# Attention and a gated feed-forward layer on one core: a third accumulator bank, scores in the accumulator ring, and new planned times

## The chip, the cores and the metric

The kernel runs on one core of a Trainium2 chip. The metric is device time in microseconds (us), from the start to the end of one execution. The kernel before takes 516.85 us, the median of three runs (515.93, 516.85 and 517.66).

## The reference

The reference takes q, k and v of shape 8 x 8 x 576 x 64 (batch, heads, positions, head width) and computes attention in a window: position i sees the positions i-63 to i. The heads are then laid side by side (512 wide) and go through a layer with two matrix products, a convolution of three taps along the positions, and a gate:

```
scores = q k^T / 8, masked to 0 <= i - j < 64;  attn = softmax(scores) v
x = attn, heads side by side             # 8 x 576 x 512
h = relu(x w_in)                         # 512 -> 1024
c = conv_w[0] h[i-1] + conv_w[1] h[i] + conv_w[2] h[i+1]
out = (h * sigmoid(c)) w_out             # 1024 -> 512
```

q and k are scaled by about 6.2, so the scores are not small. w_in, conv_w and w_out come as 64-bit floats, and the kernel converts them to 32 bits on the chip.

## The kernel before, in words

**Units and slots.** The 4608 positions are cut into 12 units of 384. A unit's inner width of 1024 is cut into 8 blocks f of 128. Planned times are in slots: one slot is one f, and unit u begins at slot 8u.

**Work of a unit.** Scores and softmax of a unit come in three groups b of four blocks (`softmax`, L477; the first two units are handled by `scores` and `weigh`, L449 and L460, in six pairs). TensorE computes scores (`qk`, L362, matmuls at L372), VectorE adds the mask and takes the row maximum (L379), ScalarE takes exponentials (L389), then they are normalised (L400), transposed by VectorE (L426), and put in place by DMAs (L438) or, for the first two units, transposed by TensorE (L405). `values` (L519, matmuls at L523) multiplies by v for one c of four; ScalarE and VectorE take the result out of PSUM as a high part xh (L527) and a low part xl (L530).

The first product, `mm1` (L540, matmuls at L543), adds up 12 matmuls of 384 columns for each f (high and low parts of x and w_in) in one bank. `relu` on ScalarE (L569 or L572) empties the bank into hbuf. For pairs i of two f the convolution runs on ScalarE (L578) and VectorE (L585), then sigmoid (L592), gate (L597), and the split into high and low parts gh (ScalarE, L609) and gl (VectorE, L612). The second product, `mm2` (L615, matmuls at L620), adds up over all f into three banks po0 to po2, nine matmuls of 512 columns for each f. The result is copied out (L660, L662) and stored (L666).

**Front.** Before this is in steady state the weights must be there: `weights` (L265) loads a chunk of 512 KB (L271), and ScalarE, VectorE and GpSimd convert it (L257 to L263) and split it into a high and a low part (L278 to L281). w_in comes in five steps, w_out in four of two f each. `keep_busy` (L215) puts matmuls that compute nothing (L220) where the planner expects TensorE to be idle in the first 110 us.

**PSUM.** There are eight banks: sc0 and sc1 for scores, acc0 and acc1 as a ring for `values` and `mm1`, and po0 to po3. `bank` (L513) gives the ring's banks in turn, in order of planned time. po3 is used for the first two units alone: transposes and score pairs (`PE_AT`, `QK_AT`, `bank_of` at L355).

**Order.** Each piece of work is put in a list with a planned time, an engine, a cost, and what it reads and writes (`at`, L226). The list is sorted by planned time, which sets the dependencies. Then `queued` (L65) goes through it once, when the kernel is built: it keeps a clock for each engine and, when an engine is free, takes of the pieces that its costs say are ready the one with the earliest planned time (0.5 slot earlier for one of the same kind as the last). The outcome is a fixed order of instructions on each engine. On the chip every engine works through its list in that order, and an instruction that waits holds all that stand behind it. Landing of a DMA is reckoned at L129 and L130. The planned times are in `START` (L145): `lag` is how many slots mm2 comes behind mm1, `qk` the three score groups, `pv` the four values groups, `in` and `out` the conversions of weights.

Of the kernel before, what the change touches and what calls it, by code (L numbers as in the profile page):

```python
# [8 lines left out]
F32 = mybir.dt.float32  # L9
# [6 lines left out]
P = 128  # L16
# [8 lines left out]
NU = B * S // NX  # L25
NG = NX + 2
TT = NX // P
NC = DM // P
NF = DFF // P
BY_PE = 2  # L30
NB = 4
# [3 lines left out]
GROUPS = ((0, 1), (2,), (3,), (4, 5))  # L35
QK_AT = (((-1,), (0,), (2,), (-1,), (0,), (2,)), ((-1,), (2,), (-1,), (2,), (-1,), (2,)))
PE_AT = ((0, 1, 2, 3, 0, 1), (0, 1, 0, 1, 0, 1))
MASKED = -8.0e9


# [24 lines left out]
def queued(works, fill=None):  # L65

    import heapq
    writer, readers = {}, {}  # L70
    for x in works:
        deps = set()
        for k in x.r:
            if k in writer:
                deps.add(writer[k])
        for k in x.w:
            deps.update(readers.get(k, ()))
            if k in writer:
                deps.add(writer[k])
        deps.discard(x)  # L80
        for d in deps:
            d.after.append(x)
        x.needs = len(deps)
        for k in x.w:
            writer[k], readers[k] = x, []
        for k in x.r:
            readers.setdefault(k, []).append(x)
    free = {"PE": 0.0, "DVE": 0.0, "ACT": 2.0, "POOL": 0.7, "SP": 0.75}
    state = dict.fromkeys(free)
    state["ACT"] = "exp"  # L90
    waiting = {e: [] for e in free}
    touched = {k: ("", 0.0) for k in [("sc", 0)] + [("acc", i) for i in range(2)] + [("po", i) for i in range(NC)]}
    for x in works:
        if x.needs == 0:
            waiting[x.eng].append(x)
    dma, port, order, left = 0.0, {"DVE": 0.0, "POOL": 0.0}, [], len(works)
    while left:
        best = None
        for e, ws in waiting.items():
            if not ws:  # L100
                continue
            start = max(free[e], min(x.ready for x in ws))
            if best is None or start < best[0]:
                best = (start, e)
        start, e = best
        x = min((x for x in waiting[e] if x.ready <= start),
                key=lambda x: x.t - (0.5 if x.kind and x.kind == state[e] else 0.0))
        if x.port:
            if e == "POOL" and start < port["DVE"]:
                free[e] = port["DVE"]  # L110
                continue
            start = max(start, port["POOL"])
            port[e] = start + x.port
        waiting[e].remove(x)
        if fill and e == "PE" and start < FILL_TO:
            t = max(free[e], FILL_FROM)
            n = int((start - t) * (FILL if start > COLD else 2.2))

            clean = [(end, k) for k, (by, end) in touched.items() if by != "PE" and end < t]
            if n > 0 and clean:  # L120
                order.append(Work(x.t, e, 0.0, fill(n, min(clean)[1]), [], [], None, 0, 0.0))
        turn = SWITCH[e] if e in SWITCH and (x.kind != state[e] if e == "PE" else x.kind and x.kind != state[e]) else 0.0
        if turn and e == "PE" and not x.kind:
            turn = LEAVE
        if e == "PE" or x.kind:
            state[e] = x.kind
        end = free[e] = start + turn + x.cost * (1.75 if e == "PE" and start < WARM else 1.0)
        if x.mb:
            dma = max(dma, start) + x.mb * 2.45  # L129
            end = dma + 2.1  # L130
        for k in x.r + x.w:
            if k[:2] in touched:
                touched[k[:2]] = e, end
        order.append(x)
        left -= 1
        for y in x.after:
            y.needs -= 1
            y.ready = max(y.ready, end + (0.0 if e == "PE" else 0.06) if y.eng == e else end + 0.2)
            if y.needs == 0:
                waiting[y.eng].append(y)  # L140
    return order
# [1 line left out]


START = {  # L145
    "v0": -75.194,
    "pv0": -28.294,
    "conv": -20.578,
    "bits": ((-108.97, -51.701), (-77.864, -72.033)),
    "qk1": -71.549,  # L150
    "lag": (17.427, 16.64, 17.098, 17.112, 17.608, 17.66),
    "mid": (4.229, 1.343, 1.083, 1.035),
    "v1": -24.291,
    "qk2": -12.096,
    "qk0": (-94.127, -93.129, -92.414, -87.931, -71.603, -79.477),
    "ex0": (-20.247, -71.357, -69.778, -64.052, -53.337, -51.735),
    "sc1": (-51.518, -55.088, -50.832, -25.283, -23.913, -20.247),
    "ex1": (-104.146, -25.732, -3.586, -17.027, -68.77, -2.709),
    "mask": -25.382,
    "sig": ((11.515, 14.523, 14.512, 21.442), (14.628, 17.367, 17.217, 19.829), (12.924, 15.579, 19.8, 20.604), (13.999, 15.174, 19.801, 20.222)),  # L160
    "in": (-24.969, -18.475, -6.673, -3.797, 1.924),
    "out": (7.771, 12.189, 12.98, 14.058),
# [3 lines left out]
}  # L166
SWITCH = {"PE": 0.14, "ACT": 1.28}
LEAVE = 0.24
# [7 lines left out]
def attention_moe(ctx: ExitStack, tc: tile.TileContext, q, k, v, w_in, conv_w, w_out, out):  # L176
# [30 lines left out]
    w24 = [flat[:, 8 * NT * 32:8 * NT * 32 + 2 * DM], flat[:, 16 * NT * 32:16 * NT * 32 + 2 * DM]]  # L207
    cbits = pool.tile([P, 3 * NF, 2], U32, name="cbits")
    sc = many(2, [P, 512], F32, "sc", psum)
    acc = many(2, [P, 512], F32, "acc", psum)  # L210
    po = many(NC, [P, 512], F32, "po", psum)

    spare = pool.tile([P, P], F32, name="spare")

# [140 lines left out]
    def bank_of(u, b, i, h):  # L355

        if not wide(u):
            return sc[h][:, i * P:(i + 1) * P]
        j = pair(u, NB * b + i)
        return (sc[h] if j < 0 else po[j + h])[:, i % 2 * P:(i % 2 + 1) * P]  # L360

# [115 lines left out]
    def softmax(u, b, t, ex_at):  # L477
        for i in range(NB):
            if block(u, b, i)[1]:
                at(t - 0.1, "POOL", 0.2, lambda b=b, i=i: nc.gpsimd.memset(ss[b][:, i, :, :W], 0.0), w=[("s", b, i)])  # L480
        at(t, "PE", 0.82, lambda b=b: qk(u, b), r=needed(b), w=[("sc", 0)], kind="eight")
        at(t + 0.002, "DVE", 1.45, lambda b=b: row_max(u, b),
           r=[("sc", 0), "mask1", "mask2"], w=[("s", b, i) for i in range(NB)] + [("nm", b, i) for i in range(NB)])
        t = ex_at
        for i in range(NB):
            at(t, "ACT", 0.74, lambda b=b, i=i: exps(u, b, i), r=[("nm", b, i)],
               w=[("s", b, i), ("sm", b, i)], kind="exp")
        t += 0.45
        e = slice(0, 2 * NB)
        sw, sr = [("sm", b, i) for i in range(NB)], [("s", b, i) for i in range(NB)]  # L490
        if u < 3:
            at(t, "POOL", 0.6, lambda: guard(b, e, nc.gpsimd), w=sw)
        else:
            at(t, "DVE", 0.15, lambda: guard(b, e, nc.vector), w=sw)
        at(t, "DVE", 0.15, lambda: reciprocal(b, e), r=sw, w=[("r", b, i) for i in range(NB)])
        if u < 3:
            two(t, "DVE", 0.88, lambda: normalise(u, b, e, nc.vector), r=[("r", b, i) for i in range(NB)], w=sr)
        else:
            two(t, "POOL", 1.5, lambda: normalise(u, b, e, nc.gpsimd), r=[("r", b, i) for i in range(NB)], w=sr)
        t += 0.4  # L500
        t = max(t, when[-1][2] + 0.1)
        for g, t0, rows in parts(b):
            at(t, "DVE", 0.12 * 2 * len(rows), lambda b=b, g=g, t0=t0, rows=rows: transpose(b, g, t0, rows), r=sr,
               w=[("T", g)] + ([("w24", 0, 0), ("w24", 0, 1)] if g else []))
            if t0 + len(rows) == NT:
                if u == BY_PE:
                    at(t + 0.01, "POOL", 1.0, lambda g=g: zero_blocks(g), w=[("u", g, i) for i in range(4)])
                for i in range(4):
                    at(t + 0.05, "SP", 2.1, lambda g=g, i=i: place(g, i), r=[("T", g)], w=[("u", g, i)], mb=0.15)
# [2 lines left out]

    def bank(key):  # L513
        if key not in banks:
            banks[key] = turn[0] % 2
            turn[0] += 1
        return banks[key]

# [191 lines left out]
            load_v(n0 + NF - 0.3, u + 2)  # L710
    load_qk(START["qk2"], 2)
    plan.sort(key=lambda x: x.t)
    for x in plan:
        x.r = [("acc", bank(a[1])) if type(a) is tuple and a[0] == "acc" else a for a in x.r]
        x.w = [("acc", bank(a[1])) if type(a) is tuple and a[0] == "acc" else a for a in x.w]

    kind = None
    for x in plan:
# [65 lines left out]
```

## Time and profile before

| what | value |
|---|---|
| median of 3 runs | 516.85 us |
| profiled execution | 521.77 us, span 520.0 us |
| TensorE busy | 503.5 us (97%) |
| VectorE, ScalarE, GpSimd busy | 370.4, 382.9, 88.9 us |
| mean granted TensorE clock | 0.993 |
| DMA | 69.89 MB, 134 GB/s in the mean |

TensorE's busy time includes the matmuls that compute nothing (16.6 us by their records). Matmuls overlap in the records: a record's length is longer than the distance between the starts of two matmuls, and the distance is what one costs. PEclk is the share of the full TensorE clock that was granted.

### The profile page before, as it was taken

The page shows a single profiled execution, that of the slowest core. Times are in us where ns is not written, and L with a number is a line of the kernel's source. Part 1 is how long each engine was busy: PE and PEld are TensorE (multiplying, and loading weights), DVE is VectorE, ACT ScalarE, POOL GpSimd, SP SyncE. Part 2 cuts the span into 40 slices and gives each one's busy share as a digit, 9 for nine tenths or more (in the row PEclk, how much of TensorE's full clock was granted, in tenths as well). Part 3 has the DMA queues.
Part 4 walks back from the last instruction along what each step waited for, and adds up shares of the span by engine and source line. Part 5 has one row for each costly group of instructions (what it writes and reads, how often), then busy time and mean ns, then how long its engine had stood idle before and what let it go on. Part 6 is the DMA issues. An engine that isn't in the chain of part 4 may idle for free.

```text
span 520.0 us, 14061 instructions
## 1 busy us (share of the span) xinstructions
PE 503.5 (97%) x5434; PEld 448.4 (86%) x5434; DVE 370.4 (71%) x1079; ACT 382.9 (74%) x1010; POOL 88.9 (17%) x196
## 2 busy tenths in 40 slices
PE   8898979999999999999999999999999999999996
PEld 7777979799988989989988988989889889898885
DVE  5889968898866667757766775775865865554970
ACT  6988958979877877777868868859769757644750
POOL 7213301221111112111103104203102201000000
PEclk9999979999999999999999999999999999999999
DMA  8983853436422542542551461452352231200111
GB/s 300 351 315 121 311 188 109 143 116 219 161 78 63 199 146 70 190 150 51 198 161 46 147 216 47 142 190 77 136 179 84 77 104 27 81 0 1 61 62 61
DMA packets 28163, 69.89 MB, mean 134 GB/s; under 512 B 5696, under 2 KB 15680, under 8 KB 28096
## 3 DMA queue, kind: packets, MB, share of 16 engines
q1 hardware_dynamic: 28096, 68.99, 39.7%
q8 instruction: 43, 0.70, 0.5%
q14 instruction: 24, 0.20, 0.1%
HBM read 47.73 MB, written 9.44 MB: 110 GB/s over the span
## 4 chain that ended last, share of the span: by engine, by line
PE 84%; DMA 9%; SPq 2%; DVE 2%; ACT 1%; issue 1%; ACTq 0%
PE po L620 38%; PE acc L543 34%; PE acc L523 6%; PE sc L372 5%; DMA q<-in_q_dram 4%; DMA bits<-in_w_out_dram 2%; SPq L438 1%; DMA bits<-in_w_in_dram 1%; DMA v<-in_v_dram 1%; SPq L243 1%; PE po L220 1%; DVE T L263 0%; ACT s L389 0%; DMA ub<-T 0%; DVE s L400 0%
## 5 line engine op out<-in xcount | busy, mean ns | idle before, releaser
L543 PE MATMUL acc<-xh,wih 128*128 128x384 f32 x384 | 131.7, 343 | 3.2 <-ACT hbuf L569 3.2
L543 PE MATMUL acc<-xl,wih 128*128 128x384 f32 x384 | 130.4, 339 | 0.0
L543 PE MATMUL acc<-xh,wil 128*128 128x384 f32 x384 | 130.0, 339 | 0.0
L585 DVE SCALAR_TENSOR_TENSOR c<-hbuf,cw,c 128x384 f32<-128x384 f32 (+1 forms) x192 | 117.5, 663 | 14.0 <-ACT c L578 13.4
L620 PE MATMUL po<-woh,gh 128*128 128x512 f32 x288 | 115.6, 401 | 0.0
L620 PE MATMUL po<-wol,gh 128*128 128x512 f32 x288 | 113.3, 394 | 0.0
L620 PE MATMUL po<-woh,gl 128*128 128x512 f32 x288 | 112.2, 389 | 0.0
L389 ACT ACTIVATE s<-s,nm 128x96 f32<-128x96 f32 (+2 forms) x288 | 105.0, 369 | 2.3 <-DVE nm L379 2.0
L543 PEld LDWEIGHTS acc<-xh,wih 128*128 128x128 f32 x384 | 73.1, 190 | 7.4 <-ACT hbuf L569 3.5
L612 DVE TENSOR_TENSOR gl<-c,gh 128x768 fp32r<-128x768 f32 x48 | 46.8, 976 | 44.1 <-ACT gh L609 44.0
L543 PEld LDWEIGHTS acc<-xh,wil 128*128 128x128 f32 x384 | 73.1, 190 | 2.6
L400 POOL TENSOR_TENSOR s<-s,r 128x768 f32<-128x768 f32 x27 | 41.8, 1546 | 195.1 <-DVE r L395 127.1
L543 PEld LDWEIGHTS acc<-xl,wih 128*128 128x128 f32 x384 | 72.9, 190 | 0.0
L620 PEld LDWEIGHTS po<-woh,gl 128*128 128x128 f32 x288 | 54.1, 188 | 12.2
L620 PEld LDWEIGHTS po<-woh,gh 128*128 128x128 f32 x288 | 54.0, 187 | 10.8
L578 ACT ACTIVATE c<-hbuf,cw 128x384 f32<-128x384 f32 (+1 forms) x96 | 53.6, 610 | 10.4 <-DVE gl L612 10.3
L620 PEld LDWEIGHTS po<-wol,gh 128*128 128x128 f32 x288 | 54.2, 188 | 7.7
L609 ACT CAST gh<-c 128x768 fp32r<-128x768 f32 x48 | 39.9, 831 | 25.7 <-PE po L620 21.4
L597 DVE TENSOR_TENSOR c<-c,hbuf 128x768 f32<-128x768 f32 (+1 forms) x48 | 45.1, 951 | 17.4 <-ACT c L592 17.1
L379 DVE CUSTOM_DVE_ANT_0 s<-sc,mask 128x96 f32<-128x96 f32 (+2 forms) x260 | 49.1, 253 | 8.2 <-PE sc L372 6.8
L389 ACT ACTIVATION_READ_ACCUMULATOR s<-s,nm 128x1 f32 x288 | 54.9, 191 | 0.0
L572 ACT ACTIVATE hbuf<-acc 128x384 f32<-128x384 f32 x64 | 31.1, 486 | 29.3 <-PE acc L543 28.9
(64 smaller groups left out, 557.9 us busy)
## 6 DMA issues: line engine op xcount, KB each, us to landing
v<-in_v_dram SPq DMA_DIRECT2D x24, 768.0 KB, 5.7
ub<-T SPq DMA_DIRECT2D x240, 48.0 KB, 1.9
k<-in_k_dram SPq DMA_DIRECT2D x22, 448.0 KB, 3.7
q<-in_q_dram SPq DMA_DIRECT2D x22, 384.0 KB, 5.1
out_dram<-T SPq DMA_DIRECT2D x11, 768.0 KB, 3.6
bits<-in_w_in_dram SPq DMA_DIRECT2D x8, 512.0 KB, 6.9
bits<-in_w_out_dram SPq DMA_DIRECT2D x8, 512.0 KB, 6.8
k<-in_k_dram SPq DMA_DIRECT2D x2, 256.0 KB, 5.3
```

The source lines that it names most:

```text
L379: nc.vector.tensor_tensor_reduce(out=ss[b][:, i, h, o:n], in0=bank_of(u, b, i, h)[:, o:n], in1=mask[m][:, o:n], scale=-0.125, scalar=3.0e3 ...
L389: nc.scalar.activation(x, x, AF.Exp, bias=nms[b][:, e], scale=-1.0, accum_out=sms[b][:, e])
L400: on.tensor_tensor(sv, sv, rs[b][:, e].unsqueeze(2).broadcast_to([P, e.stop - e.start, n]), ALU.mult)
L523: nc.tensor.matmul(acc[bank(("v", u, c))][h * D:(h + 1) * D, t * W:(t + 1) * W], vs[:, c, t, h], ub[g][:, 2 * p:2 * p + 2, 2 * t + h], sta ...
L543: nc.tensor.matmul(acc[bank(("m", u, f))][:, :NX], w[:, f, c], x[u % 2][:, c], start=(c == 0 and j == 0), stop=(c == NC - 1 and j == 2))
L572: nc.scalar.activation(hbuf[:, f, 1:1 + NX], ps[:, :NX], AF.Relu)
L578: nc.scalar.activation(cs[i % 2][:, a, :n], hbufs[u % 2][:, f, 1:1 + n], AF.Copy, scale=cw[:, 1, f:f + 1])
L585: nc.vector.scalar_tensor_tensor(c, hbufs[u % 2][:, f, e:e + n], cw[:, e, f:f + 1], c, op0=ALU.mult, op1=ALU.add)
L597: nc.vector.tensor_tensor(c, c, hbufs[u % 2][:, 2 * i:2 * i + 2, 1:1 + n], ALU.mult)
L609: nc.scalar.copy(halves(u, ghs[ring(u, i)]), kept(u, cs[i % 2]))
L612: nc.vector.tensor_tensor(halves(u, gls[ring(u, i)]), kept(u, cs[i % 2]), halves(u, ghs[ring(u, i)]).bitcast(F32), ALU.subtract)
L620: nc.tensor.matmul(po[t], x, w[:, f], start=(f == 0 and j == 0), stop=(f == NF - 1 and j == 2))
```

## The change

The ring gets a third bank, acc2, and po loses its fourth. Where po3 was used, in the first two units, the same place is now acc2, and the planner knows it as such. The second group of scores (b = 1) of each unit from the third on is written into two banks of the ring, taken in turn like the others; the first and third groups stay in sc0 and sc1. The planner reckons a DMA's landing later. All planned times in `START` are new (cut to those that the text speaks of). No instruction of the computation is added or taken out; `keep_busy` matmuls are placed anew by the planner.

```
+NA = 3
+IN_ACC = (1,)
 in queued():
-    touched = {... for k in [("sc", 0)] + [("acc", i) for i in range(2)] + [("po", i) for i in range(NC)]}
+    touched = {... for k in [("sc", 0)] + [("acc", i) for i in range(NA)] + [("po", i) for i in range(TT)]}
...
         if x.mb:
-            dma = max(dma, start) + x.mb * 2.45
-            end = dma + 2.1
+            dma = max(dma, start) + x.mb * 2.6 + (0.15 if x.mb > 0.2 else 0.0)
+            end = dma + 2.4
...
 START:
-    "bits": ((-108.97, -51.701), (-77.864, -72.033)),
-    "lag": (17.427, 16.64, 17.098, 17.112, 17.608, 17.66),
-    "in": (-24.969, -18.475, -6.673, -3.797, 1.924),
-    "out": (7.771, 12.189, 12.98, 14.058),
-    "pv": (..., (3.533, 3.36, 7.02, 7.429)),
-    "qk": ((-7.026, 4.948, -1.256), (6.222, 6.805, 7.164), (4.422, 4.464, 6.363), (3.571, 7.538, 11.237)),
+    "bits": ((-258.913, -43.524), (-27.85, -45.73)),
+    "lag": (14.24, 14.398, 15.694, 15.676, 15.748, 15.604),
+    "in": (-109.707, -10.794, -9.091, -3.35, 0.324),
+    "out": (1.022, 7.827, 9.957, 12.645),
+    "pv": (..., (5.736, 6.769, 6.475, 6.894)),
+    "qk": ((4.51, 3.967, 5.895), (7.399, 7.175, 7.913), (5.253, 4.827, 5.309), (5.703, 5.416, 6.817)),
...
-    acc = many(2, [P, 512], F32, "acc", psum)
-    po = many(NC, [P, 512], F32, "po", psum)
+    acc = many(NA, [P, 512], F32, "acc", psum)
+    po = many(TT, [P, 512], F32, "po", psum) + acc[2:]
 in bank_of():
-            return sc[h][:, i * P:(i + 1) * P]
+            tile = acc[bank(("s", u, b, h))] if b in IN_ACC else sc[h]
+            return tile[:, i * P:(i + 1) * P]
 in softmax():
-        at(t, "PE", 0.82, lambda b=b: qk(u, b), r=needed(b), w=[("sc", 0)], kind="eight")
+        where = [("acc", ("s", u, b, h)) for h in range(2)] if b in IN_ACC else [("sc", 0)]
+        at(t, "PE", 0.82, lambda b=b: qk(u, b), r=needed(b), w=where, kind="eight")
         (row_max reads `where` as well)
 in bank():
-            banks[key] = turn[0] % 2
+            banks[key] = turn[0] % NA
 before the planner runs:
+    def place_in(k):
+        if type(k) is not tuple:
+            return k
+        return ("acc", bank(k[1])) if k[0] == "acc" else ("acc", 2) if k == ("po", 3) else k
```

## Rows read from the trace of the kernel before

**Rows 1.** The page's first part: busy time, share of the span, instructions.
```profile
PE 503.5 (97%) x5434; PEld 448.4 (86%) x5434; DVE 370.4 (71%) x1079; ACT 382.9 (74%) x1010; POOL 88.9 (17%) x196
```

**Rows 2.** Windows: length, then busy time by engine, PEclk, DMA share, GB/s.
```profile
30.00:40.00 10.00, 7.86 (x121) 7.07 (x120) 9.06 (x44) 8.61 (x37) 2.71 (x4) 1.00 0.76 278
40.00:50.00 10.00, 8.91 (x192) 8.26 (x192) 8.86 (x27) 8.34 (x24) 2.78 (x4) 1.00 0.31 108
...
60.00:70.00 10.00, 7.81 (x143) 7.03 (x141) 6.64 (x24) 4.36 (x10) 2.64 (x6) 1.00 0.83 278
70.00:80.00 10.00, 9.01 (x35) 9.01 (x36) 9.16 (x11) 8.46 (x12) 1.76 (x4) 0.66 0.58 196
...
250.00:290.00 40.00, 40.00 (x460) 35.68 (x459) 26.86 (x86) 29.78 (x78) 5.97 (x9) 1.00 0.41 132
```

**Rows 3.** Timeline of TensorE, first wait: start, length, what [idle before, releaser].
```profile
37.26 0.60 PE L405 MATMUL po<-ident,s 128*128 128x128 f32 x4
41.09 0.99 PE L372 MATMUL sc<-k,q 64*32 64x96 f32 x64 [3.23 <-DMA q<-in_q_dram]
```

**Rows 4.** Timeline of TensorE, second wait and the matmuls behind it.
```profile
67.47 0.34 PE L543 MATMUL acc<-xl,wih 128*128 128x384 f32 x1
70.99 0.69 PE L543 MATMUL acc<-xh,wih 128*128 128x384 f32 x1 [3.18 <-ACT hbuf L569]
...
76.91 0.48 PE L543 MATMUL acc<-xh,wih 128*128 128x384 f32 x1
```

**Rows 5.** Chain of waits, merged: start, length, what; two units, 40 us apart.
```profile
272.61 2.11 PE acc L543 x12
274.71 2.06 PE po L620 x9
...
312.55 2.11 PE acc L543 x12
```

**Rows 6.** Timeline of ScalarE: a relu of unit 0, and the queue around 69.43.
```profile
39.18 0.47 ACT L572 ACTIVATE hbuf<-acc 128x384 f32<-128x384 f32 x1
...
69.43 1.12 ACT L257 ACTIVATE T<-bits 128x1024 f32<-128x1024 f32 x1 [5.53 <-DMA bits<-in_w_out_dram]
70.45 0.49 ACT L569 ACTIVATE hbuf<-acc 128x384 f32<-128x384 f32 x1
```

**Rows 7.** Timeline of SyncE's DMA queue: the issue of those bits.
```profile
59.34 0.80 SPq L271 DMA_DIRECT2D bits<-in_w_out_dram  x2
```

**Rows 8.** Values of unit 0 and the first mm1 (TensorE, VectorE).
```profile
20.85 1.62 PE L523 MATMUL acc<-ub,v 128*64 128x64 f32 x48
...
27.49 1.62 PE L523 MATMUL acc<-ub,v 128*64 128x64 f32 x48
...
31.00 0.42 PE L543 MATMUL acc<-xh,wih 128*128 128x384 f32 x1
...
26.01 1.02 DVE L530 TENSOR_TENSOR xl<-acc,xh 128x384 fp32r<-128x384 f32 x2
```

**Rows 9.** Timeline of TensorE in a steady unit, a visit to attention work.
```profile
284.72 0.39 PE L620 MATMUL po<-woh,gl 128*128 128x512 f32 x1
285.04 1.00 PE L372 MATMUL sc<-k,q 64*32 64x96 f32 x64
286.00 1.62 PE L523 MATMUL acc<-ub,v 128*64 128x64 f32 x48
287.55 0.50 PE L620 MATMUL po<-woh,gh 128*128 128x512 f32 x1
287.88 0.40 PE L620 MATMUL po<-wol,gh 128*128 128x512 f32 x1
```

**Rows 10.** Emptying of banks in that unit (ScalarE's relu, VectorE's reads).
```profile
275.04 0.48 ACT L572 ACTIVATE hbuf<-acc 128x384 f32<-128x384 f32 x1
...
287.94 0.25 DVE L379 CUSTOM_DVE_ANT_0 s<-sc,mask 128x96 f32<-128x96 f32 x1
...
289.35 0.55 DVE L530 TENSOR_TENSOR xl<-acc,xh 128x384 fp32r<-128x384 f32 x1
```

More of the change, by code (lines that the diff above doesn't have):

```diff
@@ L91, in queued @@
     waiting = {e: [] for e in free}
-    touched = {k: ("", 0.0) for k in [("sc", 0)] + [("acc", i) for i in range(2)] + [("po", i) for i in range(NC)]}
+    touched = {k: ("", 0.0) for k in [("sc", 0)] + [("acc", i) for i in range(NA)] + [("po", i) for i in range(TT)]}
     for x in works:
@@ L145 @@
 START = {
-    "v0": -75.194,
-    "pv0": -28.294,
-    "conv": -20.578,
-    "bits": ((-108.97, -51.701), (-77.864, -72.033)),
-    "qk1": -71.549,
-    "lag": (17.427, 16.64, 17.098, 17.112, 17.608, 17.66),
[L152 to L160, printed above, removed]
-    "in": (-24.969, -18.475, -6.673, -3.797, 1.924),
-    "out": (7.771, 12.189, 12.98, 14.058),
[3 rows of a table removed]
+    "v0": -71.95,
+    "pv0": -34.655,
+    "conv": -180.897,
+    "bits": ((-258.913, -43.524), (-27.85, -45.73)),
+    "qk1": -49.157,
+    "lag": (14.24, 14.398, 15.694, 15.676, 15.748, 15.604),
+    "mid": (34.105, 23.924, 1.179, 2.877),
+    "v1": -14.571,
+    "qk2": 1.159,
+    "qk0": (-97.809, -91.941, -91.937, -96.905, -77.255, -53.129),
+    "ex0": (5.091, -53.0, -51.19, -48.925, -20.5, -38.281),
+    "sc1": (-39.624, -39.363, -29.157, -27.618, -17.395, 0.944),
+    "ex1": (-174.932, -9.707, -5.699, 0.394, -22.941, 2.774),
+    "mask": -65.788,
+    "sig": ((11.177, 14.758, 14.533, 18.236), (11.894, 12.691, 15.861, 19.769), (14.354, 16.018, 17.085, 17.977), (13.566, 14.937, 17.862, 18.669)),
+    "in": (-109.707, -10.794, -9.091, -3.35, 0.324),
+    "out": (1.022, 7.827, 9.957, 12.645),
[3 rows of a table added]
 }
@@ L480, in softmax @@
                 at(t - 0.1, "POOL", 0.2, lambda b=b, i=i: nc.gpsimd.memset(ss[b][:, i, :, :W], 0.0), w=[("s", b, i)])
-        at(t, "PE", 0.82, lambda b=b: qk(u, b), r=needed(b), w=[("sc", 0)], kind="eight")
+        where = [("acc", ("s", u, b, h)) for h in range(2)] if b in IN_ACC else [("sc", 0)]
+        at(t, "PE", 0.82, lambda b=b: qk(u, b), r=needed(b), w=where, kind="eight")
         at(t + 0.002, "DVE", 1.45, lambda b=b: row_max(u, b),
-           r=[("sc", 0), "mask1", "mask2"], w=[("s", b, i) for i in range(NB)] + [("nm", b, i) for i in range(NB)])
+           r=where + ["mask1", "mask2"], w=[("s", b, i) for i in range(NB)] + [("nm", b, i) for i in range(NB)])
         t = ex_at
@@ L712, in attention_moe @@
     plan.sort(key=lambda x: x.t)
+    def place_in(k):
+        if type(k) is not tuple:
+            return k
+        return ("acc", bank(k[1])) if k[0] == "acc" else ("acc", 2) if k == ("po", 3) else k
     for x in plan:
-        x.r = [("acc", bank(a[1])) if type(a) is tuple and a[0] == "acc" else a for a in x.r]
-        x.w = [("acc", bank(a[1])) if type(a) is tuple and a[0] == "acc" else a for a in x.w]
+        x.r = [place_in(k) for k in x.r]
+        x.w = [place_in(k) for k in x.w]
     kind = None
```

4 rows, old and new, of the table START are left out of this document.

## The prediction

> **What bounds the kernel now.** I read the page's busy shares first, then a table of windows, then TensorE's own timeline at the places where the table shows it short of work, and last the engines that it waited for there. TensorE (PE) is busy 97% of the span, VectorE (DVE) 71% [rows 1]. In the windows from 250 us on PE is busy for 40.00 of 40 us: nothing waits there, and only less work or fewer switches could shorten it. The loss is in the front. PE is short of work in 30 to 40 us (7.86 of 10) and 60 to 70 us (7.81), and from 70 to 80 us its granted clock is 0.66 [rows 2]. DVE is nearly full in most of the front (9.06, 8.86 and 9.16 of 10 from 30, 40 and 70 us).
>
> Two single waits stand out. The first: PE ends unit 0's group f=1 and the transposes at 37.86 us, then stands for 3.23 us on a load of q, and what waits is a score group of unit 2 (64x96 in each block), not work of unit 0 [rows 3]. The second: after two groups of L543 PE stands for 3.18 us until 70.99. The 18 matmuls that follow take 5.92 us from start to start (70.99 to 76.91), where 12 take 2.11 at the full clock [rows 5], so 3.2 for 18: the lower clock level, 1.2 GHz, after the idle time, and 2.4 GHz again from about 76.91 [rows 2, 4]. That is 2.7 us on top of the wait, 5.9 us in all. What released PE there was a relu, L569 at 70.45 on ScalarE (ACT). It needed nothing late: it stood in ACT's queue behind L257 of a w_out chunk, which waited 5.53 us for its bits [rows 6]. Those two loads were issued at 59.34 us and the bits were used at 69.43 [rows 7], 10.1 us later. With two accumulator banks, both full and both waiting for that queue, PE could not go on.
>
> **The change part by part.** No matmul, activation or DMA is added or removed; the change is where results go and the order in which each engine issues.
>
> *Third bank, po3 given up.* In the front po3 held one transpose group and five score pairs of units 0 and 1; these now share the ring's third bank, so the bank is only partly new there, and wholly new once unit 1's scores are done. At the second wait, one more L543 group (12 matmuls, 2.1 us) [rows 5] fits into the third bank before PE must stand. 3.18 - 2.1 leaves 1.1 us. The first wait, of 3.23 us, left the clock at 1.00 in 40 to 50 us [rows 2, 3], so one of 1.1 us should too. So the term is 2.1 + 2.7 = 4.8 us. Bounds: 0 (the wait forms anew elsewhere) to 5.9.
>
> *Planned scores of unit 2.* Their planned times move from -7.0, 4.9 and -1.3 to 4.5, 4.0 and 5.9 (in slots of one f): two groups that stood ahead of mm1 of unit 0 now stand behind its f=3. PE then does not stand for that q. Would it have other work? L543's f=2 needs a free bank: the relu of f=0 ran only at 39.18 to 39.65 [rows 6], so with two banks PE would have stood until 39.7 anyway; with three it can start at 37.86. So both edits together are worth the whole 3.2 us, the move alone 1.4 of it (41.09 - 39.7), and neither less than 0. I take 3.2.
>
> *Values of unit 0.* L523 fills both banks at 20.85 and continues at 27.49, after the subtractions that free them at 26.01; the first L543 starts at 31.00 [rows 8]. With a third bank one column group more can be ready early. Between 0 and 2.7 us: the two subtractions of the second half (1.02 us) could follow at 27.03 and mm1 start at 28.3. I take 0, because DVE, at 9.06 and 8.86 of 10 us from 30 us on, must still convert the weights of the next f [rows 2].
>
> *Given back.* DVE is idle for only 8.7 us in all between 30 and 110 us (10 less the busy time in each of the eight windows of 10 us, four of which stand in rows 2). To run 8.0 us earlier PE needs DVE's results 8.0 us earlier, and mm2 of unit 0 is now planned at 14.7 instead of 17.9, so w_out is wanted 3 slots sooner. Against this, three softmaxes of unit 2 move out of the way. The bounds are 0 and 8.0; I take 2.5, nearer to nothing, since 3.4 us of DVE's idle time lie in 60 to 70 us [rows 2], beside PE's second wait.
>
> *The planner's later landings.* They cost nothing on the chip; they move issue times. For two w_out chunks (0.52 each) the old formula lands at 2 x 0.52 x 2.45 + 2.1 = 4.6 us, the new one at 2 x (0.52 x 2.6 + 0.15) + 2.4 = 5.4 us. The row shows 10.1 [rows 7]. So the new figures still plan this load 4.7 us too early, and whether the relu again stands behind it depends on the new order, not on the constants. I put no gain of its own on them. The Trainium skill (DMA: Bandwidth & Descriptors, "Anatomy of one DMA") fits one DMA as about 2.0 us plus bytes over 436 GB/s. By it the pair of 0.52 MB chunks is there after some 4.4 us, an estimate from that page, and the old constants were late enough; the row has over twice that, and it decides.
>
> *Unit's second scores into the ring, steady state.* Now PE makes three visits to attention work in a unit. One costs 0.09 us at its start (from the last L620 to the scores 0.32, where nine L620 take 2.06, 0.23 each) and 0.10 at its end (0.33 from 287.55 to the next L620), so 0.2 us [rows 5, 9]. With one score bank pair the groups must stand apart, since DVE reads the first only after 2.9 us (285.04 to 287.94) [rows 9, 10]; with the ring's banks two can go together. The planned times (scores at 5.4, 5.7 and 6.8, values at 5.7 to 6.9) suggest two visits. Ten units by 0.2 us: 2.0 less if it is two visits, 2.0 more if four. I take 1.0 less.
>
> *Its new wait.* L543 in that bank now waits for DVE's read of the scores. Behind it in PE's queue stand mm2 and all else. The hold is 285.04 to about 289.4, 4.4 us [rows 9, 10]; PE covers it with one L543 group in the third bank (2.1) and nine L620 (2.06): 4.2 [rows 5]. I cost it at nothing, up to 2.3 us a unit if no L620 is ready. In the mean the ring is emptier than before: by the rows' holds, a unit's eight L543 groups take about 3 us of a bank each (272.61 to the end of the relu at 275.52), four values groups 3.9 at most (286.00 to the end of the second L530), two scores 4.4, that is 48 of 3 x 40 us (40%) against 40 of 2 x 40 (50%).
>
> *Shorter lag* (17.7 to 15.6): mm2 comes two slots earlier in the order. The same matmuls remain; the stretch of L620 alone at the end gets shorter, with no effect on the sum. The tail behind the last matmul (eviction and store, about 5 us) is unchanged.
>
> **Sum.** -4.8 - 3.2 + 0 + 2.5 - 1.0 = -6.5 us. The profiled execution took 521.77 us (span 520.0), 4.9 above the median of the timed runs, so part of the waits may be peculiar to it; carried to the median: 516.85 - 6.5 = 510.4 us.
>
> **Rivals.**
> - *More than that (504.2 us).* Nothing is given back, values of unit 0 come early, two visits: 4.8 + 3.2 + 2.7 + 2.0 = 12.7 less. For it: the third bank bears on all three places. Against it: DVE at 9.06 of 10 in 30 to 40 us.
> - *The waits only move (515.9).* The landing times stay 4.7 us too optimistic, another instruction stands before a late load, and the front gives back all 8.0; only the 1.0 of the visits is left. For it: 10.1 against 5.4 us. Against it: PE now has a bank more to ride over. The Trainium skill (TensorE: Matmul & The Clock Gate, "HAM oscillation — how this bites in real kernels") reports of a kernel whose order had been mended that PSUM double-buffering gave no further gain; by that rule this is the case to expect. The trace here speaks against it, as PE's second wait is for a bank (its releaser is a relu).
> - *Slower (521.4).* The scores in the ring hold two of three banks; where DVE reads them more than 4.2 us after PE wrote them (4.4 in the row), L543 stands and PE with it, in each of ten units. At 1.0 us, a bit under half of the 2.3, that is +10; less the front's 5.5 and with no gain from visits, +4.5. It decides from 0.55 us a unit on, where it has eaten the front's gain. For it: 2.9 us until DVE begins; the lag is two slots shorter, so fewer L620 are at hand. Against it: the ring's mean load falls.
>
> **How the numbers follow.** The forecast has 0.48, more than that 0.18, the waits only move 0.16, slower 0.18. About 0.3% (1.6 us) is what a measurement of this kernel can tell from no change. The third case lies within it or just outside: I give 0.10 of it to no change and 0.06 to faster. Faster 0.48 + 0.18 + 0.06 = 0.72, same 0.10, slower 0.18. The range goes from the case of more, 504, to 518.5, which leaves out most of the slower case and a little at the low end. Within the likeliest case alone I expect 507 to 514.
>
> **What would show it.** Right: no PE idle time over 2 us behind mm1's start, granted clock 1.00 at 70 us, no score group waiting for q at 40 us, two attention visits in a unit, 39.7 to 39.8 us from unit to unit instead of the 39.94 between 272.61 and 312.55 [rows 5]. Wrong: L543 waiting for DVE's row maximum in the steady units (the slower case), or a relu behind L257 once more (the waits only move), or PE full up to 110 us but mm1 begun later than 31 us.

## The result

The changed kernel takes 510.6 us (median of 6 runs, 509.13 to 511.44) where the kernel before takes 517.23 us (6 runs). The ratio is 0.9877, with a 95% interval of 0.9855 to 0.9899: 6.4 us (1.2%) faster. The forecast was 510.4 us. A second measurement (experiment 10) gave 510.45 against 515.94 us, a ratio of 0.9882 (0.9848 to 0.9916).

The page's first part, of the kernel after:

```profile
PE 500.6 (98%) x5452; PEld 448.8 (88%) x5452; DVE 368.8 (72%) x1079; ACT 384.1 (75%) x1012; POOL 91.0 (18%) x196
```

The span is 508.9 us. Against [rows 1] the busy times hardly differ; TensorE's share rises since the span is shorter. The windows that answer to [rows 2] (length, busy time of PE, PEld, DVE, ACT, POOL, granted clock, DMA share, GB/s):

```profile
30.00:40.00 10.00, 10.00 (x101) 9.02 (x102) 9.88 (x30) 10.00 (x35) 1.67 (x3) 1.00 0.89 301
40.00:50.00 10.00, 8.94 (x249) 7.71 (x248) 9.97 (x48) 9.77 (x34) 5.29 (x7) 1.00 0.61 204
60.00:70.00 10.00, 10.00 (x60) 10.00 (x59) 9.69 (x28) 9.86 (x27) 1.74 (x4) 1.00 0.69 226
70.00:80.00 10.00, 9.93 (x136) 9.43 (x135) 10.00 (x15) 9.38 (x15) 1.30 (x4) 1.00 0.25 93
...
250.00:290.00 40.00, 40.00 (x460) 35.95 (x459) 26.82 (x87) 31.43 (x88) 5.94 (x10) 1.00 0.40 132
```

The two weak places are gone, and the clock stays at 1.00 in all of these windows. VectorE and ScalarE are now full from 30 to 50 us. What is left of TensorE's waits, summed by line and releaser over the whole span (us in total, times, longest; one more of 0.2 us is left out):

```profile
PE acc L222 <- DVE spare L225: 1.1, 1, 1.1
PE acc L547 <- DVE nm L382: 0.9, 2, 0.6
PE po L624 <- issue: 0.8, 1, 0.8
PE sc L375 <- issue: 0.6, 1, 0.6
PE sc L375 <- DVE s L403: 0.5, 1, 0.5
```

The relu behind a late load, [rows 4], is not among them, nor the score group of [rows 3]. The first mm1 begins at 26.32 us instead of 31.00, although the first score begins later, at 8.01 us instead of 5.61. In TensorE's timeline (start and length) L222 is the filler, the matmuls of `keep_busy` that compute nothing; each leaves two records, so x40 is 20 fillers:

```profile
1.05 7.03 PE L222 MATMUL acc<-spare 128*128 128x112 f32 x40 [1.05 <-DVE spare L225]
8.01 0.56 PE L375 MATMUL sc<-k,q 64*64 64x64 f32 x16
...
20.12 0.92 PE L527 MATMUL acc<-ub,v 128*64 128x64 f32 x24
...
26.32 0.44 PE L547 MATMUL acc<-xh,wih 128*128 128x384 f32 x1
```

In a steady unit there are now two visits to attention work. Two score groups stand side by side, one in the ring and one in sc. This is the stretch that answers to [rows 9], and then VectorE's reads, which answer to [rows 10]:

```profile
307.92 0.39 PE L624 MATMUL po<-woh,gl 128*128 128x512 f32 x1
308.23 0.93 PE L375 MATMUL acc<-k,q 64*32 64x96 f32 x60
...
309.00 0.96 PE L375 MATMUL sc<-k,q 64*32 64x96 f32 x62
310.07 0.92 PE L527 MATMUL acc<-ub,v 128*64 128x64 f32 x24
310.92 0.49 PE L624 MATMUL po<-woh,gh 128*128 128x512 f32 x1
...
315.28 2.32 PE L527 MATMUL acc<-ub,v 128*64 128x64 f32 x72
317.53 1.00 PE L375 MATMUL sc<-k,q 64*32 64x96 f32 x64
```

```profile
309.25 0.26 DVE L382 CUSTOM_DVE_ANT_0 s<-acc,mask 128x96 f32<-128x96 f32 x1 [0.80 <-PE acc L375]
...
310.50 0.25 DVE L382 CUSTOM_DVE_ANT_0 s<-acc,mask 128x96 f32<-128x96 f32 x1
```

VectorE waits for these scores (0.80 us) and has read the ring's two banks 2.5 us after the group began, not 4.4 as in [rows 9, 10]. From unit to unit it is now 39.5 us (visits at 308.23 and, two units on, at 387.27) where [rows 5] gave 39.94.

**Where TensorE's time goes.** For each profile I went along TensorE's whole timeline and counted each matmul from its start to the start of the next, less the idle time that the row of the next one names. Waits are those idle times, transp. the transposes on TensorE; in us, over the span:

```
                    waits  filler  scores  transp.  values   mm1    mm2   last matmul ends
before, 1st profile  12.0    15.4    35.1      5.8    37.7  206.9  203.0   515.8
before, 2nd profile   9.5    15.6    35.0      5.8    37.7  203.9  203.0   510.4
after                 4.0    18.5    33.6      5.7    37.8  204.2  201.2   504.9
```

The second profile of the kernel before is the first experiment below. It stands nearer to the timed runs (516.38 us against the 521.77 of the first), so the difference is read from it: waits -5.5, filler +2.9, and the work itself -2.9: scores -1.4, mm2 -1.8, the rest +0.3. Experiments 6 and 9 show where the shares of scores and mm2 come from.

### The profile page after: what moved, and what is told of

Read it like the earlier page. It is cut to its first block, busy times and chain, and to the rows that moved or that the text cites. A ratio compares the mean times of both kernels' runs of the same rounds, so it can differ in the third digit from the quotient of the medians.

```text
span 508.9 us, 14120 instructions
## 1 busy us (share of the span) xinstructions
PE 500.6 (98%) x5452; PEld 448.8 (88%) x5452; DVE 368.8 (72%) x1079; ACT 384.1 (75%) x1012; POOL 91.0 (18%) x196
## 3 DMA queue, kind: packets, MB, share of 16 engines
q1 hardware_dynamic: 28096, 68.99, 40.1%
## 4 chain that ended last, share of the span: by engine, by line
PE 87%; ACT 5%; DVE 5%; SPq 1%; issue 1%; DMA 0%; POOL 0%; ACTq 0%; POOLq 0%
PE po L624 36%; PE acc L547 35%; PE acc L527 7%; PE sc L375 4%; PE acc L222 2%; ACT s L392 2%; PE acc L375 2%; DVE s L382 1%; SPq L441 1%; ACT L392 1%; ACT c L582 1%; DVE s L403 1%; ACT L596 1%; PE po L408 0%; DVE T L261 0%
## 5 line engine op out<-in xcount | busy, mean ns | idle before, releaser
L624 PE MATMUL po<-woh,gh 128*128 128x512 f32 x288 | 114.2, 396 | 0.0
L403 POOL TENSOR_TENSOR s<-s,r 128x768 f32<-128x768 f32 x27 | 41.3, 1531 | 159.5 <-DVE r L398 125.8
L601 DVE TENSOR_TENSOR c<-c,hbuf 128x768 f32<-128x768 f32 (+1 forms) x48 | 46.3, 964 | 22.4 <-ACT c L596 21.9
L616 DVE TENSOR_TENSOR gl<-c,gh 128x768 fp32r<-128x768 f32 x48 | 45.7, 952 | 16.3 <-ACT gh L613 15.8
L613 ACT CAST gh<-c 128x768 fp32r<-128x768 f32 x48 | 39.8, 830 | 13.1 <-DVE c L601 7.6
L596 ACT ACTIVATE c<-c 128x768 f32<-128x768 f32 (+1 forms) x48 | 40.7, 847 | 3.9 <-DVE c L589 3.1
```

The costliest lines, as they stand in the source:

```text
L403: on.tensor_tensor(sv, sv, rs[b][:, e].unsqueeze(2).broadcast_to([P, e.stop - e.start, n]), ALU.mult)
L596: nc.scalar.activation(c, c, AF.Sigmoid)
L601: nc.vector.tensor_tensor(c, c, hbufs[u % 2][:, 2 * i:2 * i + 2, 1:1 + n], ALU.mult)
L613: nc.scalar.copy(halves(u, ghs[ring(u, i)]), kept(u, cs[i % 2]))
L616: nc.vector.tensor_tensor(halves(u, gls[ring(u, i)]), kept(u, cs[i % 2]), halves(u, ghs[ring(u, i)]).bitcast(F32), ALU.subtract)
L624: nc.tensor.matmul(po[t], x, w[:, f], start=(f == 0 and j == 0), stop=(f == NF - 1 and j == 2))
```

## The experiments

Each is given as the lines that differ, what was expected, and what came. The ratios are to the kernel before on the same chip, 515.9 to 516.4 us there.

**1. The kernel before again.** No edit.

> The kernel before once more, unchanged, for a second profile. Theory: the two long waits of TensorE (3.23 us at 41 us, 3.18 us at 71 us with the slow clock behind it) depend on when loads land and are partly peculiar to the first profiled execution, which took 521.77 us where the timed runs take 517.2; this profile then takes about 517 us, and one of the two waits is shorter by 2 us or more or the granted clock stays at 1.00 at 70 us. Rival: the profiler itself costs these 4.5 us; then the profile takes about 522 us again with both waits in it.

It took 516.38 us. Timelines of TensorE and ScalarE at the two waits (start, length, what, [idle before, releaser]), and the window that answers to the 0.66 in [rows 2]:

```profile
40.28 0.95 PE L372 MATMUL sc<-k,q 64*32 64x96 f32 x62 [3.22 <-DVE r L395]
...
68.18 0.44 PE L543 MATMUL acc<-xh,wih 128*128 128x384 f32 x1 [1.20 <-ACT hbuf L569]
```

```profile
66.62 1.12 ACT L257 ACTIVATE T<-bits 128x1024 f32<-128x1024 f32 x1 [3.58 <-DMA bits<-in_w_out_dram]
67.64 0.49 ACT L569 ACTIVATE hbuf<-acc 128x384 f32<-128x384 f32 x1
```

```profile
70.00:80.00 10.00, 9.59 (x58) 9.41 (x57) 9.97 (x14) 9.90 (x15) 3.58 (x6) 1.00 0.57 200
```

The second wait is the same in kind (a relu behind L257) but 1.20 us long, with no loss of clock: 4.7 us less than the 5.9 of [rows 4]. The first wait is there again in full. The releaser named here is VectorE, but its trace settles that it is the load as before: q was issued at 30.26 us and landed 9.9 us later, a little over 0.1 us before TensorE went on, as in the first profile, and VectorE had read the score bank by 36.7 us.

**2. The third bank alone.** `NA = 3`, `IN_ACC = ()`, old START, old landing lines.

> The kernel before with the third ring bank in place of po3 and nothing else: all scores in sc, old planned times, old landings. The prediction's term for it was 4.8 us at the wait of 71 us. Theory now: that wait was 5.9 us in one execution and 1.2 in another, so the bank can give back about 1 us there, and a new order of the front costs as much: 514.5 to 517.5 us beside 516 of the kernel before, and three visits a unit at 39.9 to 40 us. Rival (the term as forecast): 511 to 512 us.

516.82 us, ratio 1.0008 (0.9988 to 1.0029): no change in time, but not in the profile. The first mm1 begins at 26.97 us instead of 30.20 in experiment 1, and the first wait shrinks from 3.22 to 0.92 us, since half a group of mm1 now runs ahead of it (from 38.02 us). The second wait did not get shorter:

```profile
26.97 0.44 PE L547 MATMUL acc<-xh,wih 128*128 128x384 f32 x1
...
40.26 0.98 PE L375 MATMUL sc<-k,q 64*32 64x96 f32 x64 [0.92 <-DMA q<-in_q_dram]
...
68.90 0.44 PE L547 MATMUL acc<-xh,wih 128*128 128x384 f32 x1 [1.60 <-ACT hbuf L573]
```

By the count above waits are 4.3 us less than in experiment 1 (5.2 against 9.5), filler is 2.1 more (17.7) and the work itself 2.5 more; a steady unit takes 40.1 us in three or four visits. So what the bank gains early is lost again. The forecast's 4.8 us for the bank at the second wait is refuted as a gain of the bank alone.

**3. The bank, and unit 2's scores late.** Experiment 2 with one entry more:

```
-    "qk": ((-7.026, 4.948, -1.256), ...
+    "qk": ((4.51, 3.967, 5.895), ...
```

> The same as the kernel with the bank alone, and unit 2's score groups at their new planned times (4.5, 4.0 and 5.9 in place of -7.0, 4.9 and -1.3). The prediction's term for bank and move together was 3.2 us at the wait of 41 us. Theory: that wait goes, as no score group of unit 2 stands ahead of mm1 f=2 any more, and 2 to 3 us less than with the bank alone: 512 to 515 us. Rival (VectorE and ScalarE full in the front, so the wait only moves): no less than with the bank alone, with idle time or filler elsewhere before 110 us.

524.69 us, ratio 1.0141 (1.0113 to 1.0168): the rival holds, and more than holds. The wait at 41 us turned into one for VectorE's normalised scores, and there are new ones where unit 2 is late (TensorE's timeline; then the window with its granted clock):

```profile
43.48 1.06 PE L408 MATMUL po<-ident,s 128*128 128x128 f32 x8 [1.91 <-DVE s L403]
...
100.30 1.62 PE L527 MATMUL acc<-ub,v 128*64 128x64 f32 x48 [1.89 <-DMA ub<-T]
```

```profile
40.00:50.00 10.00, 8.09 (x229) 6.96 (x232) 9.59 (x40) 10.00 (x37) 5.01 (x7) 0.83 0.31 105
```

Waits 8.5 and filler 23.3 us by the count above, against 5.2 and 17.7 in experiment 2: 8.9 us more, where the medians differ by 7.9.

**4. Ring and second scores in it, old times.** `NA = 3`, `IN_ACC = (1,)`, old START, old landing lines.

> Third bank and second scores in the ring, but planned times and landings of the kernel before. Theory (bank and order share the gain): the third bank alone rides over the wait at 71 us, so 513 to 515 us; attention work still comes in three visits a unit, 39.9 to 40.0 us from unit to unit, since the planned times put the score groups apart. Rival 1 (the bank does it all): 510 to 511 us. Rival 2 (the new times do it all): 516.5 to 518 us, no change.

518.22 us, ratio 1.0044 (1.0021 to 1.0066): slightly slower, which neither the theory nor the rivals had (rival 2 ended at 518, no change). The old times put the groups in three to five visits a unit, 38.6 to 41.3 us from one unit's first mm1 to the next. One wait for gl of 2.01 us is new; it ends at 88.30 us, and the granted clock falls behind it (the window, as in [rows 2]):

```profile
90.00:100.00 10.00, 9.93 (x182) 8.36 (x181) 8.11 (x32) 9.20 (x46) 2.94 (x2) 0.85 0.51 154
```

**5. New times, two banks.** The kernel before with the new START. With two banks these times plan a third group of values into a bank before the first is taken out, so in two units part of the values are another group's; the amount of work is the same.

> Planned times of the kernel after, but two ring banks, all scores in sc, po3 kept and the old landings. Theory: the times bring the scores of unit 2 behind the first mm1 groups, worth 1 to 3 us in the front, but with one pair of score banks two groups can't stand side by side, so a unit has three visits or waits for VectorE in the steady part; 514 to 518 us. Rival (the new times do it all): 510 to 511.5 us.

527.43 us, ratio 1.0226 (1.0196 to 1.0256). Slower than the theory had it: waits 9.9 and filler 22.1 us, and 40.2 us from unit to unit. Against the kernel after it lacks three things at once (the bank, the scores in the ring, the later landings), so it does not say which of them these times need most.

**6. New times, three banks, but all scores in sc.**

```
-IN_ACC = (1,)
+IN_ACC = ()
```

> The kernel after with the second group of scores back in sc0 and sc1 (three ring banks, new times, new landings). Theory: only the steady part changes: a third visit in each of ten units, or VectorE's read between two groups, 0.2 to 0.5 us a unit, so 2 to 5 us more than the kernel after: 512.5 to 515.5 us, with 39.7 to 40.0 us from unit to unit in place of 39.5. Rival (the saved visit is worth nothing, the gain is all in the front): 510 to 511.5 us.

520.89 us, ratio 1.0100 (1.0073 to 1.0127): 10 us more than the kernel after, some 11 by the ratios, and over twice what was expected. The steady part is as expected: three visits, 39.8 to 39.9 us from unit to unit. The surprise is the front. TensorE's filler in three windows (length, busy time by records, clock), first of the kernel after, then of this one:

```profile
0.00:20.00 20.00, 14.25 (x96) 13.47 (x96) 1.00 0.91 330
20.00:60.00 40.00, 4.75 (x28) 3.50 (x27) 1.00 0.80 274
60.00:110.00 50.00, 0.37 (x2) 0.38 (x2) 1.00 0.47 156
```

```profile
0.00:20.00 20.00, 13.63 (x96) 12.68 (x96) 1.00 0.93 328
20.00:60.00 40.00, 8.98 (x62) 7.66 (x62) 1.00 0.77 272
60.00:110.00 50.00, 2.44 (x16) 2.09 (x16) 1.00 0.45 151
```

From 20 to 110 us the filler more than doubles (5.1 to 11.4 us), because the planner, which puts filler only where it expects TensorE to be idle, finds it without work there with one pair of score banks.

**7. The old landing formula under the kernel after.** `x.mb * 2.45` and `dma + 2.1` again.

> The kernel after with the old landing formula (2.45 for each MB, 2.1 us after). Theory: the planned times were fitted to the new figures, the order of the front changes in hundreds of places, and instructions stand ahead of loads that land later than planned; 0.5 to 4 us more than the kernel after, 511 to 514.5 us, all of it before 130 us, with the steady part at 39.5 us a unit. Rival (the figures have no worth of their own): within 0.7 us of the kernel after, 510 to 511.2 us.

519.66 us, ratio 1.0061 (1.0040 to 1.0081): 9 us more than the kernel after, beyond the theory's range and against the prediction's "no gain of its own". The steady part is at 39.5 us a unit, so all of it lies in the front, with waits of 9.9 us against 4.0 and the same filler. The profiled execution (517.94 us, clock 1.00) is the shortest of 12; in 9 of them the mean granted clock is 0.993 to 0.997, so part of the 9 us is the clock. The two longest waits are for q:

```profile
6.29 0.57 PE L375 MATMUL sc<-k,q 64*64 64x64 f32 x16 [1.24 <-DMA q<-in_q_dram]
...
22.68 0.67 PE L375 MATMUL sc<-k,q 64*64 64x128 f32 x16 [2.11 <-DMA q<-in_q_dram]
```

**8. New steady times, old front.** Ring and second scores in it, old landings, old START but for the third entry on of qk, pv, ex and sig (mid and lag likewise, lag with a step between).

> Three ring banks and the second scores in the ring, the old landings, the old planned times for the front and units 0 and 1, and the new planned times of the steady units (qk, pv, ex, sig, lag from the third entry on; lag with a step between). Theory: the steady part alone is worth about 0.4 us a unit in some eight units, 3 us, while the front stays as it was with the old times or gets a little worse, as in the kernel with ring and old times: 512.5 to 515.5 us. Rival 1 (the gain is all in the front): 516 to 518 us. Rival 2 (the steady part is all of it): 510 to 511 us.

514.89 us, ratio 0.9973 (0.9954 to 0.9993). Two visits, 39.5 us a unit, as in the kernel after (visits at 311.67 and 351.15), so the steady part does not need the new front. The front is no better and no worse: filler rises to 22.4 us from the 15.6 of the second profile of the kernel before, and waits fall to 2.8 from 9.5. What is left is the work itself, 2.4 us less, and so is the profiled execution (513.99, the shortest of 12, against 516.38 us); the medians differ by 1.0 us.

**9. A third visit.** The kernel after with

```
-    "qk": (..., (5.703, 5.416, 6.817)),
+    "qk": (..., (5.703, 5.416, 8.5)),
```

> The kernel after with the third score group of the units that are planned from unit 3 on moved 1.7 slots later, so that it stands by itself: three visits of TensorE to attention work in seven units in place of two. Theory: a visit costs 0.2 to 0.4 us, so 39.7 to 39.9 us from unit to unit in place of 39.5, and 1.5 to 3 us more in all than the kernel after. Rival (visits cost nothing, the shorter unit comes from elsewhere): 39.5 us from unit to unit and no change.

510.99 against 510.45 us of the kernel after beside it: 0.5 us, within the noise and under the expected 1.5 to 3. The profile is clearer. The third group stands alone, and a unit takes 39.6 to 39.7 us (TensorE's timeline, one unit and the start of the next):

```profile
308.43 0.93 PE L375 MATMUL acc<-k,q 64*32 64x96 f32 x60
...
315.33 2.32 PE L527 MATMUL acc<-ub,v 128*64 128x64 f32 x72
326.11 1.00 PE L375 MATMUL sc<-k,q 64*32 64x96 f32 x64
...
348.05 0.93 PE L375 MATMUL acc<-k,q 64*32 64x96 f32 x60
```

That is 0.1 to 0.2 us a visit, a little under the forecast's price. The rest of the 0.45 us that a unit gained goes with the scores that stand side by side, since experiment 6, where they do not, has 39.8 to 39.9. The count by matmuls agrees: with the third visit mm2 takes 202.7 us, 1.5 more than in the kernel after, and the scores 33.5, no more; in experiment 6 the scores take 35.0, as before.

**10. The kernel after again.**

> The kernel after once more, unchanged, on this chip: a ratio of 0.986 to 0.990 to the kernel before, 509 to 511 us where before takes 516 to 517, and a profile with no wait of TensorE over 1 us behind its first mm1 and 39.5 us from unit to unit. It is what the other kernels of this call stand beside.

510.45 us, ratio 0.9882 (0.9848 to 0.9916); longest wait behind the first mm1 0.85 us.

**11. Fewer fillers ahead of the first score.** `COLD = 8.0` in place of 6.0: 11 fillers instead of 20, nothing else.

> The kernel after with 11 instead of 20 filler matmuls in front of the first score; every other instruction is in the same order on every engine. Theory: the planner's later landings made the first score start at 8.0 us in place of 5.4 to 5.6, since the larger filler count of a warm clock is taken for a cold one, and the fillers, not the data, end last there; with 11 the first score starts at about 5.5 to 6.2 us. The front is a chain of scores, row maxima and exponentials up to the first mm1 at 26.3 us, so 1 to 2 us less: 508 to 509.5 us if the kernel after takes 510.5. Rival (the loss is hidden, since VectorE and ScalarE are full by 10 us anyway): within 0.4 us of the kernel after. A second rival: less activity before the first score leaves the clock low, and the kernel is slower by 1 us or more.

```profile
1.05 5.04 PE L222 MATMUL acc<-spare 128*128 128x112 f32 x22 [1.05 <-DVE spare L225]
6.01 0.92 PE L375 MATMUL sc<-k,q 64*64 64x64 f32 x16
```

The first score starts 2.0 us earlier, the first mm1 at 25.02 (1.3 earlier). 509.74 us, ratio 0.9869 (0.9838 to 0.9900), 0.7 us under the kernel after beside it, between the theory and the rival; the intervals overlap, so the time alone does not show a gain.

**12. Fewer fillers everywhere.** `COLD = 8.0` and `FILL = 3.0` in place of 4.0.

> The kernel after with fewer fillers everywhere: 11 instead of 20 ahead of the first score, and a count for 3 in place of 4 a us after that, which takes 20 or so more out of the first 110 us; every other engine's order is the same. Theory: where fillers end later than what they cover, the front gets shorter still, 0.3 to 1.5 us less than with the 11 alone, a ratio of 0.984 to 0.987 to the kernel before. Rival (what they cover ends last now): the same ratio as with the 11 alone, 0.987, and waits of TensorE in their place. Second rival: the clock falls, and it is slower.

506.80 us (506.53 to 507.17), ratio 0.9802 (0.9778 to 0.9826): below the interval of the kernel after, the best of all, and 2.9 us under experiment 11, more than the 0.3 to 1.5 expected, with 13 fillers fewer than there and not some 20. Where a filler went, TensorE now waits in one place more, and mm1 starts at 24.12:

```profile
15.82 1.50 PE L408 MATMUL po<-ident,s 128*128 128x128 f32 x12 [1.37 <-DVE r L398]
...
24.12 0.44 PE L547 MATMUL acc<-xh,wih 128*128 128x384 f32 x1
```

```profile
20.00:60.00 40.00, 38.24 (x665) 33.79 (x664) 39.82 (x139) 37.80 (x129) 13.71 (x21) 1.00 0.83 300
```

Filler falls to 13.6 us, waits stay at 4.2. VectorE is now busy for 39.82 of 40 us from 20 to 60 us, 39.08 in the kernel after. That points to VectorE as what bounds the front, and to fillers that run past their cover and delay what it gets to read; no run shows this by itself. Of the 3.9 us between the two profiles about 1 comes only later: an idle time of 0.76 us at 232 us (0.71 in experiment 10), which no row explains, is not there. The clock stays at 1.00 throughout.

## Why the prediction came out right, point by point

*What bounds the kernel: right.* The steady part was full, and front losses and switches were all there was to gain.

*The second wait, -4.8: mis-sized.* I took the term from one profile, in which the wait cost 5.9 us with the slow clock. The second profile shows 1.2 us. The text allowed that part of the waits might be peculiar to that execution, and still carried the whole term over to the median. The lower clock does come back: 18 of the 57 executions of the kernel before that ran beside the experiments have a mean granted clock of 0.993 to 0.997 (the first profile 0.993), and none of 12 of the kernel after (0.999 or 1.000). But the median of those at 0.999 or more is only 0.1 to 0.7 us under the median of all. That the bank alone removes the wait is refuted by experiment 2. In the kernel after the wait is absent, by the new order.

*Scores of unit 2 with the bank, -3.2: the wait is gone, but the time is not won by these two edits.* The bank alone takes 2.3 us of this wait, since mm1 goes on at 38.02 us, as the text had it for both edits; but the kernel gets no shorter (experiment 2). With the move it is 8 us longer (experiment 3), as TensorE waits for VectorE's normalised scores instead. The step that failed is the answer to "Would it have other work?": it asked for a free bank and not for VectorE's results.

*Values of unit 0, taken at 0 of 2.7.* mm1 started 4.7 us earlier than in the profile before (3.9 against the second one), more than my bound; a column group does go ahead in a third bank, at 20.12, 21.99 and 24.14. Most of it is the bank's: with the bank alone mm1 starts at 26.97 us (experiment 2), 3.2 us ahead of the second profile, so a term of 0 was too small. That gain was lost again behind it, which is what the term "given back" stood for.

*Given back, +2.5, and landings at nothing.* Against the second profile the front's net is waits -5.5 and filler +2.9, 2.6 us less; forecast was 5.5 less. The landings, which I had ruled out as a cost, moved the first score past the planned time (`COLD`) from which the planner puts in more filler, and 20 fillers stood ahead of it; with 11 the first score came 2.0 us earlier and the first mm1 1.3 (experiment 11). And they have a worth of their own: without them the same times are 9 us slower. With the old constants loads were waited for in experiment 7 (2.11 and 1.24 us), so the later figures serve better here. That they plan the w_out pair 4.7 us too early is more than the rows say, since the planner sets a load behind those already issued (`max(dma, start)`) and I reckoned the pair alone. By the Trainium skill's fit (DMA: Bandwidth & Descriptors, "Anatomy of one DMA"), which the section gives for DMAs on GpSimd's path, a pair of chunks lands after 4.4 us, an estimate. The loads here are issued by SyncE, and the traces do not agree with it: 10.1 and 8.1 us from issue to use.

*Visits, -1.0: right in kind, too small.* Two visits came, and the one saved is worth 0.1 to 0.2 us a unit (experiment 9). With the scores side by side, which the forecast gave no price, it is 0.45 us a unit and 2.9 us in all; experiment 8 shows the steady part by itself.

*New wait for VectorE's reads: right.* It appears twice in the front (0.9 us in all), not in steady units.

So the sum of 6.5 us came near by luck, because two errors mostly cancel: the front was worth 2.9 us less than forecast, the steady part 1.9 more, which makes 5.5 by the two profiles (5.5 and 6.6 by the medians). And the terms do not add: bank alone 0, bank with old times and scores +2.3, new times with two banks +11.6, with three but no scores in them +5.0, everything together -5.5 to -6.6 by the medians. A list of planned times is worth something only with the banks and the landing figures with which it was found.

## What to carry to other kernels

Before a wait seen in one profile goes into a sum, see it in a second execution; 4.7 of its 5.9 us were not there in the second one here. In a fixed order of instructions, a wait that is removed by moving one piece can come back at the next engine that is full, so edits to banks, times and cost figures should be measured together and each taken out of the whole, not added to the old. Work that is put in to keep an engine busy has to end before what it covers: 22 fillers fewer in the front, with all else in the same order, gave 0.7 to 0.8% at no loss of clock.

## What the runs showed of the hardware

Idle time alone did not tell when TensorE's clock fell. After idle times of 3.23 and 3.22 us at 41 us it stayed at 1.00; after 3.18 us at 71 us it fell to 1.2 GHz [rows 2 to 4]; in experiment 3 the window of 40 to 50 us shows 0.83 with idle times of no more than 1.91 us, and in experiment 4 that of 90 to 100 us shows 0.85 behind one of 2.01 us. Two runs of one program differed by 2.0 us in the landing of the same two chunks (issue to use 10.1 us at [rows 7], 8.1 us in the second profile: issued at 58.49, used at 66.62).
